# A drain of GpSimd's queue in the middle of the last tile

## The chip, the cores and the metric

The kernel runs on one core of a Trainium2 chip. The metric is the time of one execution on the device in microseconds (us). A core has five engines with a queue each: TensorE (PE; its weight loads are listed apart as PEld), VectorE (DVE), ScalarE (ACT), GpSimd (POOL) and SyncE (SP, which only issues transfers). In the profile a name with a q behind it (POOLq, SPq) is the engine's sequencer, which runs branches, semaphore instructions and drains itself.

## The reference

Three layers in a row on an input of 8 x 3072 x 256 numbers:

```
X = real(fft(fft(x, axis=1), axis=2))            # 8 x 3072 x 256 -> rows of 256
# mixture of 8 experts, one expert a row, at most `capacity` = 768 rows an expert, in order of the rows
e = argmax(X @ w_gate); g = its softmax weight
out = g * (relu(row @ w1[e]) @ w2[e])            # rows over the capacity, and their output, stay 0
h = out @ w_in
result = max(0.01 * h, h) @ w_out                # 24576 x 256
```

Only the rows that an expert keeps (8 x 768) have an output that isn't zero.

## The kernel before

The kernel computes the transform of the first batches, routes their rows to experts, and then works on 16 tiles of 384 kept rows (two for each expert). GpSimd gathers each tile's rows (`prep`, L984: three indirect transfers of 128 rows for a tile, 48 in all). The expert's two matrix products give `y`, which is put away in device memory. When all tiles have that, the second layer (the last loop of `moe_static`) runs over the 16 tiles again: a tile's `y` is loaded (`yload`, L1348), and for each of 16 blocks of 128 hidden columns `h2` computes the block (L199 to L201, with its eviction on ScalarE `gt` and VectorE `gf`, then a split in two parts `gh`, `gl`), and `o`, three blocks later (`LAG`), adds the block's share to the output (L1099, L1100). Behind a tile's last block `fin` scales the output by the gate on ScalarE and VectorE (`ob`, L1109) and GpSimd scatters it, 128 rows by an indirect transfer (L1110), three a tile, 48 in all. `fin` of a tile comes when the next tile is at its third block; the last tile's comes behind the loop. A scatter into `out` waits for the one before it, except among the last tile's three, which are declared independent. Before all that GpSimd issues one small load (`altn`, L219).

The framework writes the semaphores and plans the order of instructions on each engine with a simulated timeline. The order written in the code is kept only where the code says so: `in_order` names engines whose instructions stay in the order of the code; regions inside one another add up. Around the second layer SyncE and ScalarE are already in such a region; TensorE, VectorE and GpSimd are the planner's.

Behind the second layer the kernel reads a flag and, where the kept rows did not all come from the first batches, would run a general version of everything in `tc.If` (L1465, L1466); with these inputs it is jumped over. On the way out of the conditional each engine settles the counts of its semaphores; on GpSimd an instruction INC_SWDGE_SEM does it for the transfers that it issues itself. When the framework's context closes (L1491) GpSimd runs a DRAIN, SyncE goes through a list of waits, one for each semaphore, and a barrier over all engines ends the program.

Of the kernel before, what the change touches and what calls it, by code (L numbers as in the profile page):

```python
# [22 lines left out]
KT = T // P  # L23
NF1 = F1 // P
NF2 = F2 // P
# [118 lines left out]
class Kern:  # L144
# [1112 lines left out]
    def moe_static(self, es, tiles, rps):  # L1257

        nc = self.nc
        U = 0.173  # L1260
        cvs = ExitStack()
        self.m2 = self.pool("m2", 1, es=es)
        self.my = self.pool("my", 2, es=es)
        self.po = self.pool("po", 4, es=es, space=PSUM)
        cv = self.pool("cv", 2, es=cvs)
        self.open_wide()
        self.tr(0)
        n = len(tiles)
        steps = self.wide_steps(cv)
        wide = len(steps)  # L1270
        self.later([(c * 1.3, f) for c, f in steps])
        zq = list(range(B * S // self.ZR))
        per = -(-len(zq) // (n - 1))

        def zero(m):
            for _ in range(min(m, len(zq))):
                self.zero_step(zq.pop(0))

        def late(i, d, end):
            def go():  # L1280
                end()
                if d:
                    nc.scalar.dma_start(out=self.ysp[i], in_=self.st[i].pop("yf"))
            return go

        for i in range(n):
            e, t = tiles[i]
            new = i == 0 or tiles[i - 1][0] != e
            nxt = i + 1 < n
            wnew = nxt and tiles[i + 1][0] != e  # L1290
            for f in range(NF1):
                self.step(6 * U, 0.55, lambda: self.h(i, f))
                if new and f % 2 == 0:
                    self.conv_w2(f // 2)
                if f == 1 and i and nxt:
                    if i == 1:
                        self.upto(wide)
                    self.prep(i + 1, *tiles[i + 1])
                if f == 3 and wnew:
                    self.load_w1(tiles[i + 1][0])  # L1300
                if f == 7 and wnew:
                    self.load_w2(tiles[i + 1][0])
                if f == 6 and i:
                    zero(per)
            if nxt:
                while i + 1 not in self.st:
                    self.pop()
                self.step(0.11 * 2 * KT, 1.1, lambda: self.tr(i + 1))
            for d in range(2):
                if wnew:  # L1310
                    self.conv_w1(2 * d)
                    self.conv_w1(2 * d + 1)
                self.step(24 * U, 0.0, lambda: late(i, d, self.y(i, d, True)))
        self.upto()
        zero(len(zq))
        cvs.close()
        rps.close()
        self.mg = self.pool("mg", 4, es=es)
        self.yload(0)
        self.yload(1)  # L1320
        self.ysplit(0)
        lag = []

        def tail(m):
            while len(lag) > m:
                j, f = lag.pop(0)
                self.o(j, f)
                if f == NF2 - 1:
                    self.fin(j)

        for i in range(n):
            for f in range(NF2):
                self.h2(i, f)
                lag.append((i, f))
                tail(self.LAG)
                if f == 8 and i + 1 < n:
                    self.ysplit(i + 1)
                if f == 9 and i + 2 < n:
                    self.yload(i + 2)
        self.gsplit()  # L1340
        for k in range(KT):
            for j, f in lag:
                self.o(j, f, (k,))
            self.fin(n - 1, (k,))

    def yload(self, i):
        self.st[i]["yf"] = t = self.mg.tile([P, 2, T], F32, name="yf", tag="yf", bufs=2)
# [147 lines left out]
```

## Time and profile before

| | |
|---|---|
| median of three runs | 1030.39 us (1030.28 to 1030.99) |
| the profiled execution | 1030.87 us |
| its span, first to last instruction | 1029.1 us |
| TensorE busy | 951.8 us, 92% |
| VectorE busy | 636.4 us, 62% |
| ScalarE busy | 481.8 us, 47% |
| GpSimd busy | 126.8 us, 12% |
| granted TensorE clock, mean | 0.974 |

Busy time counts instructions of an engine proper. What a sequencer does by itself, such as a branch, a wait on a semaphore or a drain, is not counted as busy and does not stand in the list of costly groups; it shows only where one asks for the instructions of a line. The span is that of the instructions; the execution's own time has 1.8 us around it.

### The profile page before, as it was taken

What the parts mean: (1) busy time and instruction counts of PE and PEld (TensorE: products, weight loads), DVE (VectorE), ACT (ScalarE), POOL (GpSimd) and SP (SyncE); (2) the same over time, 40 slices, a digit from 0 to 9 for tenths busy, and PEclk for the clock granted to TensorE, in tenths of its full rate; (3) what the DMA queues carried; (4) which work ended last, traced back from release to release, by engine and by line L of the source; (5) the groups of instructions that cost most, each with busy time, mean ns of one, the idle gap of its engine ahead of it and who ended that gap; (6) DMA issues with size and microseconds to landing.
All of it is one profiled execution on the core that took longest, in us unless ns stands there. A gap on an engine that the chain in (4) does not pass through costs nothing. (4 is left out here: it accounts for less than half of the span.)

```text
span 1029.1 us, 15401 instructions
## 1 busy us (share of the span) xinstructions
PE 951.8 (92%) x5563; PEld 903.2 (88%) x5563; DVE 636.4 (62%) x1445; ACT 481.8 (47%) x1075; POOL 126.8 (12%) x178
## 2 busy tenths in 40 slices
PE   1749997989999999999999999999999999999993
PEld 1639996888999999998999999999999999999992
DVE  8997575979898635453555555555455555555551
ACT  4234631546665534453544444444444454445441
POOL 1000002063232221100001100110011100110011
PEclk9969997999999999999999999999999999999997
DMA  8324522479879655400000000000010000000000
GB/s 312 129 87 164 190 83 75 156 232 322 302 264 366 207 190 193 144 32 31 20 28 32 16 22 26 32 22 21 21 32 32 16 17 32 33 16 6 11 16 18
DMA packets 56192, 101.51 MB, mean 99 GB/s; under 512 B 5189, under 2 KB 39369, under 8 KB 54956
## 3 DMA queue, kind: packets, MB, share of 16 engines
q1 hardware_dynamic: 47000, 73.20, 21.1%
q0 software_dynamic: 4640, 12.81, 3.8%
q10 hardware_dynamic: 4468, 14.44, 3.5%
q8 instruction: 45, 0.74, 0.3%
q14 instruction: 39, 0.32, 0.1%
HBM read 54.54 MB, written 45.89 MB: 98 GB/s over the span
## 5 line engine op out<-in xcount | busy, mean ns | idle before, releaser
L185 DVE TENSOR_TENSOR gf<-gt,psg 128x384 f32<-128x384 f32 x256 | 141.8, 554 | 218.2 <-ACT gt L188 214.8
L188 ACT ACTIVATE gt<-psg 128x384 f32<-128x384 f32 x256 | 126.0, 492 | 253.7 <-PE psg L201 253.6
L1099 PE MATMUL po<-wo,gh 128*128 128x512 f32 x768 | 232.3, 394 | 0.0
L199 PE MATMUL psg<-yh,wi 128*128 128x384 f32 x512 | 172.7, 338 | 1.9 <-ACT yh L188 1.9
L200 PE MATMUL psg<-yl,wi 128*128 128x384 f32 x512 | 173.0, 338 | 0.0
L201 PE MATMUL psg<-yh,wi 128*128 128x384 f32 x512 | 172.7, 337 | 0.0
L185 DVE TENSOR_TENSOR gl<-gf,gh 128x384 fp32r<-128x384 f32 x256 | 141.4, 552 | 17.5 <-ACT gh L188 17.4
L1099 PEld LDWEIGHTS po<-wo,gh 128*128 128x128 f32 x768 | 139.8, 188 | 12.3
L1100 PE MATMUL po<-wo,gl 128*128 128x256 f32 x768 | 149.6, 281 | 0.0
L188 ACT ACTIVATE gh<-gf 128x384 fp32r<-128x384 f32 x256 | 132.8, 519 | 18.1 <-PE po L1099 17.8
L1100 PEld LDWEIGHTS po<-wo,gl 128*128 128x128 f32 x768 | 128.4, 188 | 4.0
L1110 POOL DMA_INDIRECT out<-ob,mix x48 | 46.9, 977 | 551.5 <-DVE ob L1109 477.9
L1042 DVE SCALAR_TENSOR_TENSOR hl<-psh,hh 128x384 fp32r<-128x384 f32 x128 | 70.0, 553 | 60.8 <-ACT hh L188 60.2
L199 PEld LDWEIGHTS psg<-yh,wi 128*128 128x128 f32 x512 | 96.6, 189 | 9.4 <-ACT yh L188 2.2
L200 PEld LDWEIGHTS psg<-yl,wi 128*128 128x128 f32 x512 | 96.8, 189 | 8.3
L201 PEld LDWEIGHTS psg<-yh,wi 128*128 128x128 f32 x512 | 96.5, 188 | 2.1
L199 PE MATMUL psy<-hh,w2h 128*128 128x384 f32 x256 | 87.9, 343 | 0.8 <-DVE hl L1042 0.8
L199 PE MATMUL psh<-xTh,w1h 128*128 128x384 f32 x256 | 86.8, 340 | 1.9 <-DVE hl L1042 1.3
L201 PE MATMUL psy<-hh,w2l 128*128 128x384 f32 x256 | 86.4, 338 | 0.0
L200 PE MATMUL psy<-hl,w2h 128*128 128x384 f32 x256 | 86.2, 337 | 0.0
L201 PE MATMUL psh<-xTh,w1l 128*128 128x384 f32 x256 | 86.0, 336 | 0.0
L200 PE MATMUL psh<-xTl,w1h 128*128 128x384 f32 x256 | 85.9, 336 | 0.0
(224 smaller groups left out, 1421.9 us busy)
## 6 DMA issues: line engine op xcount, KB each, us to landing
out<-zero SPq DMA_DIRECT2D x48, 512.0 KB, 8.8
xj<-in_xg SPq DMA_DIRECT2D x9, 1024.0 KB, 5.0
w1r<-in_w SPq DMA_DIRECT2D x9, 1024.0 KB, 7.9
w2r<-in_w SPq DMA_DIRECT2D x9, 1024.0 KB, 7.2
y_kept<-yf ACTq DMA_DIRECT2D x16, 384.0 KB, 6.2
yf<-y_kept SPq DMA_DIRECT2D x16, 384.0 KB, 3.0
y_first<-yd ACTq DMA_DIRECT2D x9, 530.0 KB, 2.8
w<-in_w_in SPq DMA_DIRECT2D x8, 512.0 KB, 5.2
```

Source lines behind the costliest of these rows:

```text
L185: self.nc.vector.tensor_tensor(out=o, in0=x, in1=y, op=op)
L188: self.nc.scalar.activation(out=o, in_=x, func=func, scale=scale)
L199: nc.tensor.matmul(out=out, lhsT=lh, rhs=rh, start=start and i == 0, stop=False)
L200: nc.tensor.matmul(out=out, lhsT=lh, rhs=rl, start=False, stop=False)
L201: nc.tensor.matmul(out=out, lhsT=ll, rhs=rh, start=False, stop=stop and i == n - 1)
L1042: nc.vector.scalar_tensor_tensor(out=lo, in0=ps[:, :T], scalar=0.0, in1=hi.bitcast(F32), op0=ALU.max, op1=ALU.subtract)
L1099: mm(out=o, lhsT=gh[:, c], rhs=both, start=f == 0, stop=False)
L1100: mm(out=o[:, :D], lhsT=gl[:, c], rhs=first, start=False, stop=f == NF2 - 1)
L1110: i = nc.gpsimd.indirect_dma_start(out=self.a["out"][0:nr], out_offset=bass.IndirectOffsetOnAxis(ap=s["ix"][:, k, 1:2], axis=0), in_=ob, i ...
```

## The change

The loop of the second layer is put into a region in which GpSimd keeps the order of the code, and in the last tile, behind its ninth block (f == 8), GpSimd gets one drain. Nothing else is changed; the lines of the loop are moved in by one level.

```
-        for i in range(n):
-            for f in range(NF2):
-                ...
+        with self.in_order("Pool"):
+            for i in range(n):
+                for f in range(NF2):
+                    self.h2(i, f)
+                    lag.append((i, f))
+                    tail(self.LAG)
+                    if f == 8 and i + 1 < n:
+                        self.ysplit(i + 1)
+                    if f == 9 and i + 2 < n:
+                        self.yload(i + 2)
+                    if f == 8 and i == n - 1:
+                        nc.gpsimd.drain()
+            self.gsplit()
+            for k in range(KT):
+                for j, f in lag:
+                    self.o(j, f, (k,))
+                self.fin(n - 1, (k,))
```

## Rows read from the trace of the kernel before

**Rows 1.** Part 4 of the page, the chain of waits: share of the span.
```profile
## 4 chain that ended last, share of the span: by engine, by line
POOL 0%; issue 0%; POOLq 0%
POOL out L1110 0%; POOLq L1466 0%
```

**Rows 2.** Busy us (instructions) of each engine in four stretches, granted clock, DMA.
```profile
core 0: us, PE busy (x) PEld busy (x) DVE busy (x) ACT busy (x) POOL busy (x), PEclk, DMA share, GB/s
978.00:990.70 12.70, 12.70 (x75) 11.86 (x74) 7.41 (x15) 6.63 (x16) 2.93 (x3) 1.00 0.06 22
990.70:1012.90 22.20, 20.62 (x119) 18.93 (x117) 11.04 (x22) 9.64 (x22) 0.01 (x1) 1.00 0.02 7
1012.90:1016.50 3.60, 0.00 (x0) 0.00 (x0) 0.00 (x0) 0.00 (x0) 2.91 (x3) 0.88 0.26 87
1016.50:1029.10 12.60, 0.00 (x0) 0.00 (x0) 0.00 (x0) 0.00 (x0) 0.00 (x0) 0.50 0.03 10
```

**Rows 3.** Line L1466 from 1016 on: duration ns min/median/max, first and last start.
```profile
L1466 POOLq EVENT_SEMAPHORE  x2: 43/43/43, 1016.5 to 1017.0; - x2
L1466 POOLq INC_SWDGE_SEM  x1: 2140/2140/2140, 1018.0 to 1018.0; - x1
```

**Rows 4.** Line L1491, 1016 to 1028.
```profile
L1491 SPq EVENT_SEMAPHORE  x12: 27/28/28, 1020.1 to 1020.8; - x12
L1491 SPq DRAIN  x2: 7/10/13, 1020.9 to 1020.9; - x2
L1491 DVEq DRAIN  x1: 17/17/17, 1016.0 to 1016.0; - x1
L1491 POOLq DRAIN  x1: 7996/7996/7996, 1020.2 to 1020.2; - x1
```

**Rows 5.** Line L1491 from 1028.2 on.
```profile
L1491 POOLq EVENT_SEMAPHORE  x4: 17/17/17, 1028.2 to 1028.9; - x4
...
L1491 POOLq DRAIN  x2: 46/78/109, 1028.4 to 1028.8; - x2
```

**Rows 6.** Line L1482, the program's start, GpSimd.
```profile
L1482 POOLq INC_SWDGE_SEM  x1: 27/27/27, 0.1 to 0.1; - x1
...
L1482 POOLq DRAIN  x1: 169/169/169, 0.3 to 0.3; - x1
```

**Rows 7.** DMA issues of GpSimd: count, median us to landing.
```profile
xg<-y_first,mix POOLq DMA_INDIRECT x48, 4.1
out<-ob,mix POOLq DMA_INDIRECT x48, 2.4
altn<-in_altn POOLq DMA_DIRECT2D x1, 1.5 KB, 5.2
```

**Rows 8.** Timeline of GpSimd from 978 on: start, us, instruction, idle before and releaser.
```profile
982.53 0.98 POOL L1110 DMA_INDIRECT out<-ob,mix  x1 [26.20 <-DVE ob L1109]
985.71 0.98 POOL L1110 DMA_INDIRECT out<-ob,mix  x1 [2.21 <-DVE gl L185]
989.69 0.98 POOL L1110 DMA_INDIRECT out<-ob,mix  x1 [3.00 <-DMA out<-ob,mix]
1012.88 0.97 POOL L1110 DMA_INDIRECT out<-ob,mix  x1 [22.22 <-DVE ob L1109]
1014.16 0.98 POOL L1110 DMA_INDIRECT out<-ob,mix  x1 [0.30 <-issue]
1015.45 0.98 POOL L1110 DMA_INDIRECT out<-ob,mix  x1 [0.30 <-issue]
```

**Rows 9.** Line L1110 over the whole second layer, the scatters.
```profile
L1110 POOL DMA_INDIRECT out<-ob,mix x48: 975/975/1042, 512.7 to 1015.4; - x48
...
L1110 POOLq EVENT_SEMAPHORE  x45: 17/17/20028, 515.2 to 992.1; - x45
...
DMA to landing us min/median/max: 2.4/2.4/4.1
```

**Rows 10.** Timeline of ScalarE in the last tile: the evictions of steps 8 and 15.
```profile
992.56 0.49 ACT L188 ACTIVATE gt<-psg 128x384 f32<-128x384 f32 x1 [1.19 <-PE psg L201]
...
1007.24 0.49 ACT L188 ACTIVATE gt<-psg 128x384 f32<-128x384 f32 x1 [1.20 <-PE psg L201]
```

**Rows 11.** Timeline of all engines behind the last matmuls.
```profile
1010.80 0.52 PE L1100 MATMUL po<-wo,gl 128*128 128x256 f32 x3
...
1011.63 1.27 DVE L1109 SCALAR_TENSOR_TENSOR ob<-po,gate,ob 128x256 f32<-128x256 f32 x3 [2.16 <-ACT ob L188]
```

**Rows 12.** Groups by line, 505 to 1012: busy us, mean ns | idle us before.
```profile
L1099 PE MATMUL po<-wo,gh 128*128 128x512 f32 x729 | 220.9, 394 | 0.0
L200 PE MATMUL psg<-yl,wi 128*128 128x384 f32 x479 | 161.3, 337 | 0.0
```

More of the change, by code (lines that the diff above doesn't have):

```diff
@@ L1329, in tail @@
                     self.fin(j)
-        for i in range(n):
-            for f in range(NF2):
[L1333 to L1344, printed above, removed]
+        with self.in_order("Pool"):
[15 more added lines that the diff above has]
+                self.fin(n - 1, (k,))
     def yload(self, i):
```

## The prediction

> **What bounds the kernel now.** I read the chain of waits first, because it names what ended last: it stops at the last scatter and is almost empty [rows 1]. That is not a kernel without a critical path; it says that what stands behind the scatter is sequencer work, which this view doesn't follow. So next the busy table by stretches [rows 2]: TensorE works without a gap until 1011, GpSimd issues its last three scatters from 1012.9 to 1016.4, and in the last 12.6 us no engine does anything that counts as work. That stretch is 1.2% of the span. What fills it is found by asking for the lines of the conditional and of the closing of the framework's context, sequencers included. INC_SWDGE_SEM starts at 1018.0, takes 2.14 us, ends at about 1020.2 [rows 3]. GpSimd's DRAIN starts at 1020.2 and takes 8.00 us, to 1028.2 [rows 4]. The closing barrier takes the rest, 1028.2 to 1029.1 [rows 5]. SyncE walks its own closing list from 1020.1 and is through at 1020.9 [rows 4]; from then on only the DRAIN is missing.
>
> Why 8.0 us? Two further drains of the same engine follow at 1028.4 and 1028.8 and take 0.109 and 0.046 us [rows 5], and one at the start, before GpSimd has issued a transfer, takes 0.169 [rows 6]. Waiting for data isn't it: INC_SWDGE_SEM stands behind a wait for the last scatter, so by 1018.0 everything had landed. What tells the long drain from the short ones is what lies in front of it: 97 transfers issued by GpSimd, 48 gathers, 48 scatters and one load [rows 7], and no drain between them and the end. My reading: a drain works through each transfer since the last drain once. (7.996 - 0.109) / 97 = 0.081 us for each.
>
> **The change, part by part.** *The drain in the middle.* On GpSimd's queue it stands behind the third scatter of the last tile but one (issued 989.69 to 990.67) and ahead of the last tile's first (1012.88) [rows 8]; the written order sees to that. It has 94 of the 97 transfers in front of it (97 less the last three): 0.109 + 94 x 0.081 = 7.7 us. It can't finish before the newest scatter has landed: a scatter lands 2.4 us after its issue at the median, 4.1 at most [rows 9], so 992.1 to 993.8. If, in addition, it were held until the step behind which it is written, that is step 8 of 16: the evictions of steps 8 and 15 start at 992.56 and 1007.24 (7 x 2.1 us apart) [rows 10], the same time again. So it runs from about 992 to 1000 or 1002. Queued behind it on GpSimd are only the last three scatters, whose data come at 1012.1 (the first of three updates, from 1011.63, 0.48 us long each) [rows 11]; GpSimd already waits there, 20.0 us on a semaphore [rows 9]. Cover left over: 10 us or more, cost nothing. Without that cover each us would push the three scatters, and with them the end, by one us. Its own length, which no row in the middle shows, lies between 0.046 us [rows 5] and 8.00 [rows 4] unless something there holds it up (rival D); either end is covered.
>
> *The end drain.* Three transfers are left to it: 0.109 + 3 x 0.081 = 0.35 us. The bounds are 0.046 [rows 5] and 8.00 [rows 4], no gain; I take 0.35, which lies by the row with nothing outstanding, since 3 of 97 is close to nothing. The gain is not 7.6 us, though: behind it SyncE is late next, with 0.8 us of list from the end of INC_SWDGE_SEM [rows 4]. The stretch from there to the barrier shrinks from 8.1 us (1020.1 to 1028.2) to 0.8: 7.3 us.
>
> *INC_SWDGE_SEM.* It is GpSimd's too and handles the same transfers' semaphores: 2.14 us with 97 issued, 0.027 at the start with none [rows 3, 6]. Those are the two bounds. In proportion to the three that are left it would take 0.027 + 3/97 x 2.11 = 0.09; but the instruction at the end may have more to do than the one at the start, one semaphore after another, and SyncE's entries at 0.028 us each [rows 4] put eight of them at 0.2. Together 0.3, near the lower row as the drain is. Gain 1.8 us.
>
> *The order stated in the second layer.* GpSimd has nothing there but the 48 scatters, which stand in the order of the code already [rows 8, 9]. Nothing is moved past SyncE's or ScalarE's queue. The planner sees one instruction more and could set other engines differently; TensorE has 0.0 us of idle time in front of its two dominant groups in this layer [rows 12], so a better order has nothing to win and a worse one would show as idle time. So the bounds are 0, since without idle time there is nothing to gain, and +2.1 us, one step of the pipeline [rows 10] run empty, an estimate; I take 0, by the row without idle time.
>
> **Sum**, against the profiled execution: 1030.87 (span 1029.1 and 1.8 around it) - 7.3 - 1.8 = 1021.8. The profiled run is 0.48 above the median 1030.39, so 1021.3 for a median: 0.9% faster, span about 1020.0.
>
> **Against a page.** The end drain's row shows 8.0 us on an engine idle since 1016.4 [rows 2, 4]. The Trainium skill, "PSUM — Partial Sum Buffer", section "Engine vs sequencer instructions", says that a drain waits for the engine to go fully idle. By that alone the end drain should have been as short as the 0.109 us one, and a drain in the middle would leave the end as it is: 1030.4. The trace speaks against it as the whole story; the rival is below.
>
> **Rivals.**
> *A: the drain's share goes, INC_SWDGE_SEM stays at 2.14 us.* For it: it waits on a semaphore and writes semaphores, and nothing shows that it looks at old transfers. Against it: 0.027 us at the start. Time: 1030.39 - 7.3 = 1023.1.
> *B: no change.* The 8.0 us belong to the end (what INC_SWDGE_SEM or the closing leaves behind), or a drain in the middle does not settle what the end drain looks at, so the change doesn't do what it says. For it: the long drain is the first one behind INC_SWDGE_SEM, and no drain in this trace stands between transfers. Against it: the two short drains follow the same INC_SWDGE_SEM. Time 1030.4.
> *C: part of the 8.0 us is a fixed price of draining after any transfer*, say half: the end drain takes 4 us, and with INC_SWDGE_SEM at 0.3 to 2.14 the time is 1030.39 - (8.1 - 4.0) - 1.8 to 0 = 1024.5 to 1026.3.
> *D: slower.* In the middle the drain runs beside a busy VectorE (11.0 of 22.2 us in that stretch), at the end beside none [rows 2]. If VectorE's work holds it up, its 7.7 us stretch. It has from 992.1 to 1012.7 free, 20.6 us, and wins 9.1 at the end; it makes the kernel slower from 29.7 us on, a factor of 3.9. At a factor of 5 it ends at 992.1 + 38.5 = 1030.6, the first scatter moves from 1012.9 by 17.9 us, less 9.1: 1039.2. Against it: the scatters' issue takes 0.98 us beside a busy VectorE and 0.98 with it idle (1015.45) [rows 8].
> The Trainium skill, "SBUF — State Buffer", section "SBUF: two separate sides", says that GpSimd and some VectorE instructions lock each other out of a shared pair of ports, and names a case of 620 ns that became 3100. That is D's rule; the two equal issue times speak against it here.
>
> **How the numbers follow.** The forecast with INC_SWDGE_SEM between 0.03 and 1 us 0.66 (1021.0 to 1022.0), A 0.14, C 0.06, B 0.09, D 0.05 (with it whatever else the planner may do). About 0.2%, 2.1 us, is what a measurement of this kernel can tell from no change. Faster: forecast, A and C, 0.86; same: B, 0.09; slower 0.05. The range takes in the forecast, with half a microsecond below it for the spread of runs (the three shown lie 0.7 us apart), the step that the planner could cost (1021.3 + 2.1 = 1023.4), and A with the same spread: 1020.5 to 1023.8. Left out are C, B and D, 0.2.
>
> **What would show it.** Right: a GpSimd DRAIN of 7 to 8 us starting between 990 and 993, ending well before 1012; the end drain under 0.5 us; INC_SWDGE_SEM under 1 us; the barrier starting some 0.8 us behind it, released by SyncE; scatters still at 1012.9, 1014.2, 1015.4. Wrong: an end drain that is still some microseconds long (C, B); INC_SWDGE_SEM still 2.1 (A); a first scatter of the last tile later than 1013 (D); TensorE's last matmul at another time than 1011.3 (the planner).

## The result and the profile after

| | before | changed |
|---|---|---|
| median of six runs each | 1030.34 us (1029.26 to 1030.99) | 1020.61 us (1019.79 to 1021.97) |
| the profiled execution | 1030.87 us | 1019.98 us |
| its span | 1029.1 us | 1018.1 us |

The ratio is 0.9908, with a 95% interval from 0.9895 to 0.9921: the kernel is 0.9% faster, 9.7 us by the medians and 8.1 to 10.8 by the interval. A second round (e5) gave 0.9916 (0.9902 to 0.9929).

The busy table of the changed kernel, in stretches that answer to [rows 2] (columns as there). The lines and times have moved: the closing of the context is now L1494, the conditional L1469, the new drain L1342, and this execution was 1.8 us ahead before the changed code began to matter.

```profile
976.00:988.50 12.50, 12.50 (x73) 11.70 (x72) 7.40 (x15) 6.52 (x15) 2.10 (x3) 1.00 0.07 22
988.50:1011.00 22.50, 21.00 (x121) 19.23 (x119) 10.94 (x22) 9.87 (x22) 0.83 (x1) 1.00 0.02 7
1011.00:1014.70 3.70, 0.00 (x0) 0.00 (x0) 0.08 (x1) 0.00 (x0) 2.93 (x3) 0.86 0.27 85
1014.70:1018.10 3.40, 0.00 (x0) 0.00 (x0) 0.00 (x0) 0.00 (x0) 0.00 (x0) 0.50 0.11 40
```

The stretch in which no engine works has shrunk from 12.6 to 3.4 us. The others, cut by hand, agree within 0.3 us, and the last matmul and the three scatters stand where they stood, each 1.8 us ahead. What fills the last stretch, by the line of the conditional and that of the closing (as [rows 3, 4]):

```profile
L1469 POOLq INC_SWDGE_SEM  x1: 260/260/260, 1016.2 to 1016.2; - x1
```

```profile
L1494 SPq EVENT_SEMAPHORE  x12: 28/28/28, 1016.4 to 1017.1; - x12
L1494 SPq DRAIN  x2: 7/10/13, 1017.2 to 1017.2; - x2
L1494 POOLq DRAIN  x1: 303/303/303, 1016.5 to 1016.5; - x1
```

INC_SWDGE_SEM takes 0.26 us instead of 2.14 and the end drain 0.303 instead of 7.996. The drain is through at 1016.8, SyncE's list only at 1017.2: SyncE is what the barrier now waits for. Where the 9 us of work went is seen at the new line, and that nothing waited for it in GpSimd's timeline (as [rows 8]):

```profile
L1342 POOLq DRAIN  x1: 8957/8957/8957, 988.1 to 988.1; - x1
```

```profile
988.35 0.98 POOL L1110 DMA_INDIRECT out<-ob,mix  x1 [3.48 <-DMA out<-ob,mix]
1011.08 0.98 POOL L1110 DMA_INDIRECT out<-ob,mix  x1 [21.75 <-DVE ob L1109]
1012.36 0.98 POOL L1110 DMA_INDIRECT out<-ob,mix  x1 [0.30 <-issue]
1013.64 0.98 POOL L1110 DMA_INDIRECT out<-ob,mix  x1 [0.30 <-issue]
```

It runs from 988.1 to 997.1; the next scatter still waits for VectorE's data until 1011.08. TensorE's last matmul ends at 1009.51 (before: 1011.32 [rows 11]), and its groups in the layer still have no idle time in front (as [rows 12]):

```profile
1008.99 0.52 PE L1100 MATMUL po<-wo,gl 128*128 128x256 f32 x3
...
L1099 PE MATMUL po<-wo,gh 128*128 128x512 f32 x726 | 220.0, 394 | 0.0
L200 PE MATMUL psg<-yl,wi 128*128 128x384 f32 x478 | 161.0, 337 | 0.0
```

### The profile page after: what moved, and what is told of

Its sections match the earlier page's. It is cut to its first block, busy times and chain, and to the rows that moved or that the text cites. A ratio compares the mean times of both kernels' runs of the same rounds, so it can differ in the third digit from the quotient of the medians.

```text
span 1018.1 us, 15402 instructions
## 1 busy us (share of the span) xinstructions
PE 952.1 (94%) x5563; PEld 904.3 (89%) x5563; DVE 636.4 (63%) x1445; ACT 480.9 (47%) x1075; POOL 130.8 (13%) x178
## 5 line engine op out<-in xcount | busy, mean ns | idle before, releaser
L1110 POOL DMA_INDIRECT out<-ob,mix x48 | 47.0, 979 | 551.5 <-DVE ob L1109 475.8
```

What stands on the lines that cost most here:

```text
L1110: i = nc.gpsimd.indirect_dma_start(out=self.a["out"][0:nr], out_offset=bass.IndirectOffsetOnAxis(ap=s["ix"][:, k, 1:2], axis=0), in_=ob, i ...
```

## The experiments

Ratios are to the kernel before, run beside each kernel on the same chip. In the sums n is the number of transfers that GpSimd has issued since its drain before (in the code it is the number of tiles).

### One half of the change alone

**e1: the order without the drain.** Edit to the changed kernel:

```
-                    if f == 8 and i == n - 1:
-                        nc.gpsimd.drain()
```

> The second layer in the region that keeps GpSimd's order, without the drain. Theory (a drain works through each transfer that GpSimd issued since the last drain, some 0.082 us each, and INC_SWDGE_SEM does so too, 0.02 us each; the order is worth nothing): as before, 1030.3 us, end drain 8.0 us, INC_SWDGE_SEM 2.1. Rival (the stated order changed the plan of the other engines and a part of the gain is its): faster than before by 0.5 us or more, TensorE's last matmul earlier counted from the layer's first.

Measured: 1030.79 us, ratio 1.0004 (0.9994 to 1.0015); end drain 7.996 us, INC_SWDGE_SEM 2.14, the same to the nanosecond as before. The stated order by itself is worth nothing.

**e2: the drain without the order.** The kernel before, with the drain in its loop:

```
                 if f == 9 and i + 2 < n:
                     self.yload(i + 2)
+                if f == 8 and i == n - 1:
+                    nc.gpsimd.drain()
```

> The drain without the stated order, so that the planner places it. Theory: what counts is only how many transfers stand behind it on GpSimd's queue. At the place of the changed kernel: 1020.6 us, end drain 0.30. Placed ahead of the first scatter: 48 left, end drain 0.06 + 48 x 0.082 = 4.0, INC_SWDGE_SEM 1.2, 1024.7 us. Placed ahead of every gather: 1030.3, end drain 8.0. Rival (the order is needed for the plan, not only for the place): slower than these at the same place.

Measured: 1029.22 us, ratio 0.9995 (0.9985 to 1.0004). The planner put the drain at the very start, as its line shows (duration ns, first and last start):

```profile
L1341 POOLq DRAIN  x1: 4522/4522/4522, 2.3 to 2.3; - x1
```

Only one transfer, the small load, was in front of it there. 96 were left, and the end drain took 7.906 us, 0.09 less than before; INC_SWDGE_SEM 2.12, 0.02 less. The third of the expected cases, near enough: without the order there is no gain. The drain reads and writes no tile, so no data hold it in its place, and the planner put it where it is of no use.

**e3: the drain in the first tile, in the region.** `i == n - 1` became `i == 0`.

> The drain in the first tile of the second layer instead of the last: 49 transfers in front of it (48 gathers, 1 load), 48 scatters behind. Theory: it takes 0.06 + 49 x 0.082 = 4.1 us, the end drain 4.0, INC_SWDGE_SEM 0.2 + 48 x 0.02 = 1.2; 1020.6 + 3.2 + 0.9 = 1024.7 us. Rival 1 (only scatters into the output count): end drain 8.0, 1030.3. Rival 2 (a price paid once, by the first drain behind any transfer): end drain 0.3, 1020.6.

Measured: 1029.72 us, ratio 0.9995 (0.9985 to 1.0005); end drain 7.906 us. The place that I took for granted did not hold: this drain, too, ran at 2.3 us. The region keeps the order among GpSimd's own instructions inside it; in the first tile none of its scatters stands ahead of the drain, and against the gathers, which are outside, the planner may move it. So this run says the same as e2, and does not decide between the theory and its rivals. (Read by itself, its 7.9 us would have spoken for "only scatters count".)

### How the price goes

**e9: the drain in the ninth tile.** `i == n - 1` became `i == 8`; the scatters of eight tiles now hold it in place.

> The drain in the ninth tile of the second layer, behind the scatters of eight tiles, which the region puts ahead of it: 73 transfers in front (48 gathers, 1 load, 24 scatters), 24 behind. Theory (price by transfers not yet drained): it takes 1.25 + 73 x 0.082 = 7.2 us beside other work, the end drain 0.06 + 24 x 0.082 = 2.0 us, INC_SWDGE_SEM 0.2 + 24 x 0.02 = 0.7; 1020.8 + 1.3 + 0.4 = 1022.5 us. Rival (a price paid once): 1020.8.

```profile
L1342 POOLq DRAIN  x1: 7242/7242/7242, 751.4 to 751.4; - x1
```

```profile
L1494 POOLq DRAIN  x3: 46/109/2018, 1016.4 to 1019.0; - x3
```

Measured: 1023.05 us, ratio 0.9926 (0.9905 to 0.9947); the new drain 7.24 us, the end drain 2.018, INC_SWDGE_SEM 0.68. Each of the three as expected. A price paid once is out.

**e10: the same number of transfers, fewer rows.** The kernel of e1 with

```
-                ap=s["ix"][:, k, 1:2] ... in_=ob
+                ap=s["ix"][:16, k, 1:2] ... in_=ob[:16]
```

> No drain in the middle; each of the 48 scatters writes 16 of its 128 rows (the output lacks the others). Still 97 transfers, with 57% of the rows. Theory (by transfers): end drain 8.0 us, INC_SWDGE_SEM 2.1. Rival (by rows or bytes): end drain 4.6 us.

Measured: 1030.57 us, ratio 1.0006 (0.9990 to 1.0022); end drain 7.996 us, INC_SWDGE_SEM 2.14, unchanged. The price goes by transfers, not by what they move.

**e4, e11, e12: more transfers.** No drain in the middle; behind the scatter in `fin`:

```
+            if self.slots is not None and key != last tile:      # e11: key < 6, e12: key < 9
+                nc.gpsimd.indirect_dma_start(... ap=s["ix"][:16, k, 1:2] ... in_=ob[:16] ...)
```

> No drain in the middle; behind each scatter of the first 15 tiles a second one that writes 16 of its 128 rows once more (45 more transfers, 142 in all, 6% more rows). Theory (the price goes by transfers): end drain 0.06 + 142 x 0.082 = 11.7 us, INC_SWDGE_SEM 0.2 + 142 x 0.02 = 3.0; 1030.3 + 3.7 + 0.9 = 1034.9 us. Rival (it goes by rows or bytes): end drain 8.5 us, 1031.

Measured: 1022.47 us, ratio 0.9934 (0.9916 to 0.9952): faster than before, where the theory said 4.6 us slower.

```profile
L1497 POOLq DRAIN  x3: 46/109/1789, 1016.5 to 1018.8; - x3
```

The end drain took 1.789 us, not 11.7, and INC_SWDGE_SEM 0.61, not 3.0. Both are close to what the theory gives for 21 transfers (1.78 and 0.62). So either the theory was wrong, or 121 of the 142 had been settled on the way, without a drain. Two counts below 142 tell these apart.

> No drain in the middle; the second small scatter of 16 rows only in the first six tiles: 18 more, 115 transfers, 2% more rows. Theory (by transfers, and what was seen with 142 is an emptying that comes at the 122nd): end drain 0.06 + 115 x 0.082 = 9.5 us, INC_SWDGE_SEM 2.5; 1029.9 + 1.5 + 0.4 = 1031.8 us. Rival (small transfers cost nothing or make the others cheap): end drain 8.0 us or less, 1030 or less.

```profile
L1497 POOLq DRAIN  x3: 46/109/9466, 1017.8 to 1027.8; - x3
```

Measured: 1032.05 us, ratio 1.0020 (1.0007 to 1.0033); end drain 9.466 us, INC_SWDGE_SEM 2.50.

> No drain in the middle; the second small scatter in the first nine tiles: 27 more, 124 transfers. With 142 the end looked like 21 left over, so 121 had been settled somewhere. Theory (it comes by itself when a 122nd transfer is issued): 3 left, end drain 0.3 us, INC_SWDGE_SEM 0.26; 1020.8 us without any drain in the middle. Rival (no emptying at that count, or one by rows or by time): end drain 0.06 + 124 x 0.082 = 10.2 us, 1032.7, or a number between.

```profile
L1497 POOLq DRAIN  x3: 46/109/10203, 1020.7 to 1031.5; - x3
```

Measured: 1032.69 us, ratio 1.0017 (1.0007 to 1.0027); end drain 10.203 us, INC_SWDGE_SEM 2.68. The guess that the emptying comes with the 122nd transfer was wrong; its rival held. Up to 124 the price keeps growing by the transfer.

What all kernels but e4 left for the end, beside the line 0.303 + 0.0818 x (n - 3), drawn through the changed kernel and the one before ((7.996 - 0.303) / 94 = 0.0818):

| transfers left (n) | kernel | end drain us | line | INC_SWDGE_SEM us |
|---|---|---|---|---|
| 2 | e6 | 0.222 | 0.221 | 0.24 |
| 3 | changed, e5, e8 | 0.303 | | 0.26 |
| 3 | e7 | 0.293 | 0.303 | 0.26 |
| 24 | e9 | 2.018 | 2.021 | 0.68 |
| 96 | e2, e3 | 7.906 | 7.910 | 2.12 |
| 97 | before, e1, e10 | 7.996 | | 2.14 |
| 115 | e11 | 9.466 | 9.465 | 2.50 |
| 124 | e12 | 10.203 | 10.201 | 2.68 |

INC_SWDGE_SEM is 0.20 + 0.02 x n in every row.

### Where the drain stands

**e5: the changed kernel again**, for the next three.

> The changed kernel once more, as the comparison for the three that follow. 1020.6 us.

Measured: 1020.99 us, the ratio given above.

**e6: the drain without cover.** Taken from the loop and put behind the first of the last three scatters:

```
                 self.fin(n - 1, (k,))
+                if k == 0:
+                    nc.gpsimd.drain()
```

> The drain behind the first of the last tile's three scatters, where nothing covers it: 95 transfers in front, 2 behind. Theory: it takes 7.8 us or, with the landing of the newest, up to 9, and pushes the two scatters behind it; last landing some 7.6 us later than in the changed kernel, end drain 0.2: 1028.2 us. Rival (the drain costs little wherever it stands, and what the change saved came from something else): 1020.6.

Measured: 1028.99 us, ratio 0.9996 (0.9986 to 1.0005): the gain is gone. GpSimd's timeline shows the drain (1012.0 to 1021.0, 9.04 us) as idle time between the first scatter and the second:

```profile
1012.21 0.98 POOL L1110 DMA_INDIRECT out<-ob,mix  x1 [21.67 <-DVE ob L1109]
1021.82 0.98 POOL L1110 DMA_INDIRECT out<-ob,mix  x1 [8.63 <-issue]
1023.10 0.98 POOL L1110 DMA_INDIRECT out<-ob,mix  x1 [0.30 <-issue]
```

**e7: a drain in every tile.** `if f == 8 and i == n - 1` became `if f == 8`.

> A drain in each of the 16 tiles. Theory: the first takes 4.1 us (49 transfers), each of the others 0.06 + 3 x 0.082 = 0.3 us, all beside other work; the end is that of the changed kernel: 1020.6 us. Rival (a drain has a price of its own, or holds up other engines): slower by 15 times that price.

```profile
L1342 POOLq DRAIN  x16: 2789/2804/5430, 2.3 to 990.3; - x16
```

Measured: 1021.77 us, ratio 0.9920 (0.9902 to 0.9939), beside 0.9916 for one drain. Fifteen more drains can't be told from none. Again the first ran at 2.3 us; the second, in the second tile, had 51 transfers and took 5.43 us. The other fourteen, each with three scatters in front, take 2.8 us and not the 0.3 expected. So the 48 gathers among the 51 count too, which e3 was to show. The fourteen start 0.2 us before the tile's newest scatter and end 2.6 us behind its start, when it has landed (2.4 us at the median [rows 9]).

### A version that goes on from there

**e8: TensorE's order stated for the loop behind the layer.**

```
-            for k in range(KT):
+            with self.in_order("PE"):
+                for k in range(KT):
                     ...
```

> The changed kernel, with TensorE's order stated too for the last three blocks of the last tile (the loop behind the layer), so that the first 128 rows are done before the second and the third. The planner now mixes the three, and all three updates and scatters stand behind the last matmul: 1.28 us from scatter to scatter. Theory (what stands behind the last matmul sets the end): first scatter 2 us earlier, last matmul up to 0.6 us later (TensorE waits for the last block's split), last scatter 1.2 us earlier: 1019.4 us. Rival (TensorE's wait eats it): 1020.6 or more.

Measured: 1019.59 us, ratio 0.9902 (0.9886 to 0.9917), against 0.9916 (0.9902 to 0.9929) for the changed kernel beside it. By time alone the two are not told apart. The traces show the step. In the changed kernel (e5) the last matmuls and what follows are

```profile
1010.46 0.52 PE L1100 MATMUL po<-wo,gl 128*128 128x256 f32 x3
1010.77 1.20 ACT L188 ACTIVATE ob<-po,gate 128x256 f32<-128x256 f32 x3 [2.24 <-PE po L1100]
...
1015.11 0.98 POOL L1110 DMA_INDIRECT out<-ob,mix  x1 [0.30 <-issue]
```

and in e8

```profile
1008.09 0.47 ACT L188 ACTIVATE ob<-po,gate 128x256 f32<-128x256 f32 x1 [1.07 <-PE po L1100]
...
1009.86 0.98 POOL L1110 DMA_INDIRECT out<-ob,mix  x1 [20.72 <-DVE ob L1109]
1009.89 0.28 PE L1100 MATMUL po<-wo,gl 128*128 128x256 f32 x1
...
1012.43 0.98 POOL L1110 DMA_INDIRECT out<-ob,mix  x1 [0.30 <-POOLq L1470]
```

The last scatter starts 4.1 us behind the last matmul's end in e5 (1010.98 to 1015.11) and 2.3 us behind it in e8 (1010.17 to 1012.43), because the first is issued before TensorE is done. TensorE pays some of that back with two waits for the last block's split in e8 (0.40 and 0.38 us, for `gl`).

## Why the prediction was right

**The end.** From the start of INC_SWDGE_SEM to the end of the span it was 11.1 us before (1018.0 to 1029.1) and is 1.9 us now (1016.2 to 1018.1): 9.2 us, against 9.1 forecast. INC_SWDGE_SEM 0.26 against 0.3, the end drain 0.303 against 0.35, and SyncE's list last, 0.8 us, as forecast. The reading of the closing lines as work that goes by transfers since the last drain holds over seven counts from 2 to 124. The medians moved by 9.7; the half microsecond beyond the 9.2 is inside the interval, and the second round's 0.9916 is 8.6 us. That 1020.61 came out near the lower end of the range (1020.5) is the spread of runs, as far as the traces show, and no part of the mechanism. INC_SWDGE_SEM's 0.3 was right in size without a shown reason: the line's fixed part is 0.20 us, as large as the eight entries of SyncE's that the sum borrowed, but no run shows that it consists of eight semaphores.

**The drain in the middle** was mis-sized, at no cost: 8.96 us from 988.1, not 7.7 from 992. Its length is over the bound of 8.00 that the prediction set, and outside the 7 to 8 us named as a sign of being right; its start, 1.8 us later in the time of the kernel before, is 989.9, just ahead of the 990 to 993 named. My sum let it begin when the newest scatter has landed. It begins as soon as GpSimd's sequencer reaches it, 0.2 us before that scatter starts. e9, e7's second and e6 (73, 51, 95 transfers; 7.24, 5.43, 9.04 us) and this one (94) lie within 0.02 us of 1.25 + 0.082 x n. The 1.25 us answer to the newest scatter's issue: 0.2 us until it starts, 0.98 us that it takes, and the 0.06 us of the end drain's line. So the sizes fit a drain that waits out that issue and then goes through the transfers while the newest is still under way; had it waited for the landing, it would have taken some 0.2 + 2.4 + 7.7 = 10.3 us. The wait for the issue is the part of a drain that the Trainium skill, "PSUM — Partial Sum Buffer", section "Engine vs sequencer instructions", tells of, a wait for the engine to be idle; the larger part, by transfers, is not in that rule, and the 7.996 us on an idle engine [rows 2, 4] show it alone.

**The order** is worth 0 as a plan (e1), as forecast, and everything as a fence (e2). That "the written order sees to that" was right for the last tile, and would have been wrong for the first (e3).

**The rivals.** A (INC_SWDGE_SEM stays) is out by 0.26 us and by seven counts; B by the result; C (a fixed share) by the changed kernel's 0.303 us and by e6 and e9, whose end drains lie on a line that meets 0.06 us at no transfer. D (VectorE holds the drain up) by e9 against e6: 73 transfers beside a busy VectorE (3.69 of 7.20 us) and 95 with every other engine idle have the same price each.

```profile
core 0: us, PE busy (x) PEld busy (x) DVE busy (x) ACT busy (x) POOL busy (x), PEclk, DMA share, GB/s
751.40:758.60 7.20, 7.20 (x44) 6.77 (x43) 3.69 (x8) 3.45 (x7) 0.98 (x1) 1.00 0.05 18
...
1012.60:1021.00 8.40, 0.00 (x0) 0.00 (x0) 0.00 (x0) 0.00 (x0) 0.59 (x1) 0.70 0.07 20
```

The first row is e9's drain, the second e6's from 1012.6 on. The Trainium skill's lock-out ("SBUF — State Buffer", section "SBUF: two separate sides") does not show in a drain here.

**What stays open:** why 142 transfers left a price as of 21. It needs more than 124. At 0.082 us each 121 would be 9.9 us, and from the 125th on no transfer of GpSimd's in that trace takes over 1.2 us; only its waits are long enough. What settled the 121, and when, no run shows. There is one lead. In e4 the 129th transfer in order of issue (the 14th from the last) starts 3.36 us behind the end of the one before it, released by nothing that the profile names, where most of the doublings (L1114) wait 1.7 us for a landing:

```profile
950.56 0.86 POOL L1114 DMA_INDIRECT out<-ob,mix  x1 [3.36 <-issue]
953.37 0.98 POOL L1110 DMA_INDIRECT out<-ob,mix  x1 [1.96 <-DMA out<-ob,mix]
956.07 0.86 POOL L1114 DMA_INDIRECT out<-ob,mix  x1 [1.72 <-DMA out<-ob,mix]
```

If 121 of the first 128 were settled there, the 7 left and the 14 from the 129th on would make the 21. Waits of about that size stand before scatters elsewhere too (3.00 us at 989.69 [rows 8]), so this is where to look next, and not a cause that is shown. Nor does any run show what a drain does for each transfer, only that each is paid for once.

## What to carry to other kernels

Where a trace has a stretch at its end in which no engine is busy, ask for the sequencers' instructions of the closing lines: here 10 us of 12.6 were bookkeeping for transfers that GpSimd had issued long before. If GpSimd waits somewhere for tens of microseconds anyway, a drain there settles that bookkeeping in hiding; count the transfers in front of it and make sure that its end lies ahead of GpSimd's next needed issue, for uncovered it gives the whole gain back. An instruction without data needs other instructions in front of it that the stated order holds there (e3 lacked them), and where the planner put it is read from the trace, not from the code.

## What the runs showed of the hardware

Each transfer that GpSimd has issued since its last drain costs 0.082 us in the next drain and 0.02 us in INC_SWDGE_SEM, whether it moved 16 rows or 128 (e10); gathers count too (e7's second drain). This held from 2 to 124 transfers. Not expected: a drain behind a scatter that is just being issued takes 1.25 us + 0.082 us each (51 to 95 transfers), so it does not wait for that one's landing before it works on the others; with only three to work on it lasted until the newest had landed (e7's 2.8 us). With 142 transfers the end drain was as short as for 21, without a drain before it (e4); with 124 it was not (e12).
